# Half of an up projection rewritten as a Strassen scheme over batch pairs, its sums spread over three engines

## The chip, the cores and the metric

One core of one Trainium2 chip. Times are device microseconds of one execution. The program uses a single core, so an execution has no second core to be compared with; all runs named here agreed within 0.3% of their median unless a range is given, and the record marks all of them as fast (no run fell into a slower state that would have to be set apart). "PE" is TensorE (matmuls), "PEld" its weight loads, "DVE" VectorE, "ACT" ScalarE, "POOL" GpSimd. "L1201" in a profile line is line 1201 of the kernel's file; the lines that matter are named in words as they come.

## The reference

Eight batches of block-causal attention, and behind it a mixer with one product over tokens and one over channels:

```python
B, H, S, D = 8, 8, 576, 64                   # DM = 512, d_tok = 256, d_ch = 1536
attn = softmax(block_causal(q @ k.T / sqrt(D)))        # blocks of 64
x = (attn @ v) as (B, 576, 512)
h = relu(x.T @ w_tok1) @ w_tok2              # token mixing
u = x + h.T
h2 = relu(u @ w_ch1) @ w_ch2                 # "up" 512 -> 1536, "down" 1536 -> 512
return (u + h2).astype(float32)
```

## The kernel before

A plan in Python simulates the engines, decides once in which order every instruction is issued, and then emits them in that order; each engine runs its own queue in order. So TensorE waits wherever the next instruction of its queue isn't ready, even if a later one is. The up projection multiplies each of twelve chunks of 128 channels by the 512 columns of a batch, four matmuls of 512 columns a chunk, and one ReLU takes the result out of PSUM:

```python
sc = ring(2, [128, 2, 512], FP32, "sc", psum)   # attention's scores: two PSUM tiles of two banks
mm = ring(4, [128, 512], FP32, "mm", psum)      # everything else: four tiles of one bank
BANK = ("mm",)
def bank_of(note):
    return mm[note["slot"]]
...
def channel_up(b, uT_done, wc1_ready, prio):
    for cc in range(NDC):                        # 12 chunks
        def emit(o, cc=cc, bank=bank):
            for m in range(NDM):                 # 4 matmuls
                nc.tensor.matmul(out=bank_of(bank), lhsT=wc1_sb[:, m, channels(cc)],
                                 rhs=uT[b % 2][:, :, m, :], start=(m == 0), stop=(m == NDM - 1))
        ...
        relu(o, gT[b % 2][:, cc, :], bank_of(bank))      # ScalarE or VectorE
```

The down projection is already a seven-product (Strassen-like) scheme. Four sums of 768 bf16 columns are made on VectorE for each half batch, and seven products are folded out of PSUM one after the other:

```python
def channel_down_fast(b, g_done, wc2_ready, u_done, prio):
    for t in range(2):
        for key, dst, x, y, op in (("s1", s1, a21, a22, ADD), ("s2", s2, s1, a11, SUB),
                                   ("s4", s4, a12, s2, SUB), ("s3", a21, a11, a21, SUB)):
            nc.vector.tensor_tensor(out=dst, in0=x, in1=y, op=op)
        ...  # 7 products of 6 matmuls of 256 columns, each folded by VectorE into an fp32 tile
```

The softmax here doesn't subtract the row's maximum and nothing guards it: scores larger than these inputs give would overflow.

## Time and profile before

| | before |
|---|---|
| time, median of 3 (range) | 298.75 us (298.72 to 298.76) |
| span in the profile | 296.9 us |
| last product of attention ends | 197.9 us |
| last matmul ends | 293.5 us |
| waits of TensorE after start-up | none over 0.3 us |
| granted TensorE clock | full in all 40 slices |
| GpSimd after attention | idle |

TensorE is the bound: what it has to stream sets the end, and the other engines only have to stay out of its way. The prediction below shows the lines of the profile for that.

### The profile page before, as it was taken

The page shows a single profiled execution, that of the slowest core. Times are in us where ns is not written, and L with a number is a line of the kernel's source. Part 1 is how long each engine was busy: PE and PEld are TensorE (multiplying, and loading weights), DVE is VectorE, ACT ScalarE, POOL GpSimd, SP SyncE. Part 2 cuts the span into 40 slices and gives each one's busy share as a digit, 9 for nine tenths or more (in the row PEclk, how much of TensorE's full clock was granted, in tenths as well). Part 3 has the DMA queues.
Part 4 walks back from the last instruction along what each step waited for, and adds up shares of the span by engine and source line. Part 5 has one row for each costly group of instructions (what it writes and reads, how often), then busy time and mean ns, then how long its engine had stood idle before and what let it go on. Part 6 is the DMA issues. An engine that isn't in the chain of part 4 may idle for free.

```text
span 296.9 us, 7686 instructions
## 1 busy us (share of the span) xinstructions
PE 290.8 (98%) x3257; PEld 184.7 (62%) x3276; DVE 203.7 (69%) x509; ACT 164.4 (55%) x233; POOL 62.0 (21%) x96
## 2 busy tenths in 40 slices
PE   8999999999999999999999999999999999999995
PEld 3576456465557855546764567774586677558774
DVE  5566879899679979959988787665086085028284
ACT  5896755578767566686666664624612611670400
POOL 9776363701700070340040000000000000000000
PEclk9999999999999999999999999999999999999999
DMA  9999999992992299991239022211033043100314
GB/s 210 183 196 202 212 182 189 222 215 66 163 133 41 42 137 203 198 131 35 41 56 168 2 20 53 91 47 62 2 71 144 0 91 109 68 2 0 145 31 148
DMA packets 64387, 31.99 MB, mean 108 GB/s; under 512 B 53088, under 2 KB 55008, under 8 KB 64352
## 3 DMA queue, kind: packets, MB, share of 16 engines
q0 software_dynamic: 44320, 17.34, 49.0%
q1 hardware_dynamic: 19744, 13.57, 17.4%
q8 instruction: 25, 0.41, 0.5%
q10 hardware_dynamic: 288, 0.59, 0.5%
q14 instruction: 10, 0.08, 0.1%
HBM read 35.85 MB, written 9.44 MB: 153 GB/s over the span
## 4 chain that ended last, share of the span: by engine, by line
PE 95%; DMA 2%; DVE 1%; ACT 1%; issue 1%; ACTq 0%
PE mm L950 28%; PE mm L1049 22%; PE mm L558 10%; PE sc L511 10%; PE mm L1144 7%; PE mm L739 6%; PE mm L832 4%; PE mm L977 4%; DMA gT<-in_q_dram 2%; PE mm L863 1%; ACT e_sb L530 1%; PE mm L783 1%; PE mm L335 0%; PE mm L913 0%; DVE u_sb L847 0%
## 5 line engine op out<-in xcount | busy, mean ns | idle before, releaser
L530 ACT ACTIVATE e_sb<-sc 128x1024 bf16<-128x1024 f32 x95 | 92.6, 1028 | 30.8 <-PE sc L511 30.5
L950 PE MATMUL mm<-uT,wc_sb 128*128 128x512 bf16 x384 | 89.6, 380 | 0.0
L725 ACT ACTIVATE gT<-mm 128x512 bf16<-128x512 f32 x76 | 45.4, 597 | 64.8 <-PE mm L950 53.9
L950 PEld LDWEIGHTS <-wc_sb 128*128 128x128 bf16 x384 | 41.7, 114 | 37.1 <-issue 3.6
L425 POOL DMA_DIRECT2D v<-in_v_dram x45 | 37.1, 837 | 33.5 <-PE mm L1049 22.4
L1049 PEld LDWEIGHTS <-gT 128*128 128x128 bf16 x336 | 32.0, 98 | 6.7 <-issue 1.7
L511 PE MATMUL sc<-qT,kT 32*128 32x64 bf16 (+4 forms) x744 | 35.4, 281 | 0.4 <-DVE qT L396 0.3
L558 PEld LDWEIGHTS <-e_sb 128*128 128x128 bf16 x896 | 31.5, 97 | 6.6 <-issue 3.1
L558 PE MATMUL mm<-v,e_sb 128*128 128x65 bf16 x896 | 34.3, 193 | 0.0
L586 DVE TENSOR_TENSOR x_sb<-mm,rinv 128x320 bf16<-128x320 f32 x64 | 31.2, 491 | 2.2
L1032 DVE TENSOR_TENSOR sums<-gT 128x768 bf16<-128x768 bf16 x14 | 7.2, 555 | 36.4 <-ACT gT L725 36.4
L1071 DVE TENSOR_TENSOR o_sb<-mm,u_sb 128x256 f32<-128x256 f32 x56 | 23.1, 420 | 7.7 <-PE mm L1049 6.8
L1049 PEld LDWEIGHTS <-sums 128*128 128x128 bf16 x252 | 24.3, 98 | 5.6 <-DVE e_sb L536 0.4
L847 DVE TENSOR_TENSOR u_sb<-mm,x_sb 128x512 bf16<-128x512 f32 x28 | 17.8, 685 | 7.9 <-PE mm L832 6.6
L511 PEld LDWEIGHTS <-kT 32*128 32x128 bf16 x752 | 12.4, 93 | 17.1 <-issue 13.8
L1071 DVE TENSOR_TENSOR o_sb<-mm,o_sb 128x256 f32<-128x256 f32 x42 | 17.4, 421 | 7.5 <-PE mm L1049 7.1
L396 DVE STREAM_TRANSPOSE kT<-kraw 128x288 int32<-128x288 int32 x32 | 21.0, 705 | 1.8 <-ACT kraw L356 1.6
L1049 PE MATMUL mm<-wc_sb,gT 128*128 128x256 bf16 x168 | 22.0, 273 | 0.0
L1049 PE MATMUL mm<-wd_sb,gT 128*128 128x256 bf16 x168 | 21.9, 273 | 0.0
L1049 PE MATMUL mm<-wd_sb,sums 128*128 128x256 bf16 x168 | 21.4, 273 | 0.0
L396 DVE STREAM_TRANSPOSE qT<-qraw 128x288 int32<-128x288 int32 x32 | 21.0, 705 | 0.6 <-PE sc L511 0.3
L727 DVE TENSOR_SCALAR gT<-mm 128x512 bf16<-128x512 f32 x20 | 13.8, 688 | 7.6 <-PE mm L950 7.2
(78 smaller groups left out, 285.2 us busy)
## 6 DMA issues: line engine op xcount, KB each, us to landing
out_dram<-o_sb SPq DMA_DIRECT2D x15, 512.0 KB, 3.2
qraw<-in_q_dram POOLq DMA_DIRECT2D x15, 288.0 KB, 7.1
kraw<-in_k_dram POOLq DMA_DIRECT2D x15, 288.0 KB, 6.8
v<-in_v_dram POOLq DMA_DIRECT2D x28, 128.0 KB, 6.7
wc_sb<-in_moe_w_ch_dram POOLq DMA_DIRECT2D x8, 192.0 KB, 7.2
wc_sb<-in_moe_w_ch_dram POOLq DMA_DIRECT2D x3, 512.0 KB, 10.8
out_dram<-o_sb SPq DMA_DIRECT2D x10, 128.0 KB, 2.4
v<-in_v_dram POOLq DMA_DIRECT2D x15, 64.0 KB, 5.9
```

What stands on the lines that cost most here:

```text
L396: nc.vector.transpose(dst[:, 0:S, :] .rearrange("p s e -> p (s e)") .bitcast(I32) .rearrange("p (a k) -> p k a", k=NB)[:, k0:k1], raw2.bit ...
L425: nc.gpsimd.dma_start(out=dst, in_=src)
L511: nc.tensor.matmul(out=home(n)[:, c0 : c0 + w], lhsT=kT[i][r, j0 : j0 + 128, par], rhs=qT[i][r, i0 : i0 + w, par], start=(par == 0), stop= ...
L530: nc.scalar.activation(dst, sc[SC.index(note["pool"])][:, :, 0:n], EXP, scale=scale)
L558: nc.tensor.matmul(out=u[:, I, 0:65], lhsT=w, rhs=vt[:, J, head, 0:65], start=(J == 0), stop=(J == I),)
L586: nc.vector.tensor_tensor(out=xt[:, :, 64 * head : 64 * head + 64], in0=u[:, :, 0:64], in1=ri.to_broadcast([128, 5, 64]), op=MULT,)
L725: nc.scalar.activation(dst, src, RELU)
L739: nc.tensor.matmul(out=bank_of(bank)[:, w * n : w * n + w], lhsT=wt[:, tt : tt + 255 : 2], rhs=xt[:, c, cols], start=(c == 0), stop=(c == 4),)
L950: nc.tensor.matmul(out=bank_of(bank), lhsT=wc1_sb[:, m, channels(cc)], rhs=uT[b % 2][:, :, m, :], start=(m == 0), stop=(m == NDM - 1),)
L1049: nc.tensor.matmul(out=bank_of(bank)[:, 0:256], lhsT=x[:, kk], rhs=y[:, kk], start=first and kk == 0, stop=kk == H6 - 1, skip_group_check= ...
L1071: nc.vector.tensor_tensor(out=dst, in0=bank_of(bank)[:, 0:256], in1=other, op=ADD)
L1144: nc.tensor.matmul(out=ps, lhsT=gt[:, cc, c0 : c0 + 128], rhs=wc2_sb[:, cc, cols], start=(cc == 0 and not turned), stop=(cc == NDC - 1),)
```

## The change

Intent: take an eighth of the up projection's matmuls away for batches 4 to 7. Two batches form the two column blocks of one matrix product, and seven products of two matmuls replace eight. Four sums of weights (once) and four of the data (per pair) have to be made first, and the products have to be joined: three copies out of PSUM, three additions and some ReLUs for every group of four output chunks. The new sums lie in buffers that attention no longer needs (`raws` held the loads of q and k). To spare VectorE, GpSimd makes the weight sums, some of the down projection's sums and some residual additions; ScalarE copies for the latter. The eight PSUM banks, four of which served the scores, serve everything once the last scores are read. The diff (cuts are marked `...`):

```diff
-    qraw = ring(3, [128, NB, D], BF16, "qraw")
-    kraw = ring(3, [128, NB, D], BF16, "kraw")
+    raws = sb.tile([128, 6, NB * D], BF16, name="raws")
+    ws_sb = raws....                             # weight sums, once q and k are done with
 ...
-    BANK = ("mm",)
+    P.pool("late", [])
+    BANK = ("mm", "late")
     def bank_of(note):
-        return mm[note["slot"]]
+        n = note["slot"]
+        return mm[n] if note["pool"] == "mm" else sc[n // 2][:, n % 2]
 ...
+    def up_weight_sums(wc1_ready):
+        for dst, x, y, op in ((w[0], a21, a22, ADD), (w[1], w[0], a11, SUB),
+                              (w[2], a11, a21, SUB), (w[3], a12, w[1], SUB)):
+            def emit(o, dst=dst, x=x, y=y, op=op):
+                (nc.vector if o.engine == "DVE" else nc.gpsimd).tensor_tensor(out=dst, in0=x, in1=y, op=op)
+            prev = [P.add("POOL", 4.0, emit, deps + prev, 20.0)]                  # L1054
 ...
+    def channel_up_fast(b, uT_done, wc1_ready, prio):
+        ...                                      # 4 data sums on VectorE: L1070
+        for n in range(NDC // 2):                # 6 groups
+            # product(): 2 matmuls, L1100; keep(): copy out of PSUM, L1119; join(): L1128; clip(): ReLU in SBUF
 ...
     def channel_down_fast(...):
-                    nc.vector.tensor_tensor(out=dst, in0=x, in1=y, op=op)
+                    (nc.vector if o.engine == "DVE" else nc.gpsimd).tensor_tensor(...)    # L1201
-                    "DVE", dve_cost(768, 2), emit, ...
+                    ("DVE", "POOL") if 2 <= b < B - 1 else "DVE", ...
+                if residual and not final and FAST_UP <= b < B - 1:
+                    nc.scalar.copy(dst, bank_of(bank)[:, 0:256])                          # L1242
+                    nc.gpsimd.tensor_tensor(out=dst, in0=dst, in1=other, op=ADD)          # L1247
```

## The prediction

> **What bounds the kernel now.** I read the page first, then the chain of waits in order of time, then the waits of TensorE, then busy time by stretches, then the groups kept apart by shape.
>
> ```profile
> span 296.9 us, 7686 instructions
> PE 290.8 (98%) x3257; PEld 184.7 (62%) x3276; DVE 203.7 (69%) x509; ACT 164.4 (55%) x233; POOL 62.0 (21%) x96
> PE 95%; DMA 2%; DVE 1%; ACT 1%; issue 1%; ACTq 0%
> ```
>
> The third line is the engine summary of the chain that ended last: 95% of the span is TensorE. A busy PE alone proves little, because matmuls overlap, so I look at the spacing in the chain and at what PE waited for.
>
> ```profile
> 205.58 7.03 PE mm L950 x32
> 250.90 15.54 PE mm L950 x72
> 266.44 9.17 PE mm L1049 x84
> 286.29 7.22 PE mm L1049 x66
> PE mm L328 <- DVE wd_sb L299: 1.2, 1, 1.2
> PE sc L511 <- DVE qT L396: 0.3, 1, 0.3
> ```
>
> L950 is the up projection with 512 columns: 15.54 / 72 = 0.216 us a matmul. L1049 is the down projection, already a seven-product scheme, with 256 columns: 9.17 / 84 = 0.109 us. The last two lines are all of PE's recorded waits: 1.5 us, both at the start. So PE streams columns almost without a hole, and the time moves only if columns go away or holes appear.
>
> ```profile
> 203.00:230.00 27.00, 26.95 (x180) 17.59 (x180) 13.55 (x29) 10.53 (x18) 0.00 (x0) 1.00 0.21 59
> 230.00:260.00 30.00, 29.95 (x205) 19.81 (x204) 10.16 (x23) 12.53 (x22) 0.00 (x0) 1.00 0.25 66
> 260.00:290.00 30.00, 29.95 (x243) 22.40 (x243) 16.83 (x39) 9.18 (x16) 0.00 (x0) 1.00 0.14 45
> ```
>
> Columns: stretch, length, busy PE, PEld, DVE, ACT, POOL, granted clock, DMA share, GB/s. Attention has ended by 203 us; from there VectorE is busy 13.55 + 10.16 + 16.83 = 40.5 of 87 us (47%), ScalarE 32.2 (37%), GpSimd not at all. This is where the change puts its additions, and they have idle engines to go to.
>
> ```profile
> L725 ACT ACTIVATE gT<-mm 128x512 bf16<-128x512 f32 x76 | 45.4, 597 | 64.8 <-PE mm L950 53.9 <-DVE o_sb L1071 10.7
> L727 DVE TENSOR_SCALAR gT<-mm 128x512 bf16<-128x512 f32 x20 | 13.8, 688 | 7.6 <-PE mm L950 7.2
> L1032 DVE TENSOR_TENSOR sums<-gT,sums 128x768 bf16<-128x768 bf16 x14 | 7.4, 549 | 0.0
> L1009 DVE TENSOR_TENSOR wd_sb<-wc_sb,wd_sb 128x1536 bf16<-128x1536 bf16 x2 | 1.9, 953 | 0.0
> L1071 DVE TENSOR_TENSOR o_sb<-mm,o_sb 128x256 f32<-128x256 f32 x42 | 17.4, 421 | 7.5 <-PE mm L1049 7.1
> 200.96 2.48 DVE L847 TENSOR_TENSOR u_sb<-mm,x_sb 128x512 bf16<-128x512 f32 x4 [1.66 <-PE mm L832]
> ```
>
> These rows are the price list. The last one, from the timeline, adds one thing: four 512-column additions in a row take 2.48 us, so each costs the queue 0.62 us though one alone lasts 0.685.
>
> **What the Trainium skill says.** "TensorE: Matmul & The Clock Gate", section Back-to-back issue gap, gives N/2.4 + 2.5 ns for the warm gap: 216 ns at 512 columns. The trace agrees (215.8). "VectorE: DVE Perf Modes", section on the perf-mode tier table, caps a tensor_tensor at two elements a cycle in bf16 from SBUF and one with a PSUM operand. The trace agrees: from 768 to 1536 bf16 columns 549 becomes 953 ns (0.53 ns a column), from 256 to 512 columns out of PSUM 421 becomes 685 (1.03 ns). "GPSIMD Engine Reference", section 3.1, puts a two-input addition at about 2.6 cycles an element at 1.2 GHz; GpSimd adds nothing in this trace, so no run here shows it. "SBUF — State Buffer", section Who interferes with whom, says a VectorE instruction with two SBUF inputs and a GpSimd instruction that reads SBUF exclude each other, the later one waiting for the whole of the earlier. Nothing in this trace tests it either.
>
> **The change, part by part.**
> Removed, PE: for each of two batch pairs, two batches times 12 chunks times 4 matmuls = 96 become 6 groups of 7 products of 2 matmuls = 84. That is 2 x 12 = 24 matmuls of 512 columns less, 24 x 0.216 = **5.2 us**, all in the stage after attention, where PE is the chain. It is one eighth of half the up projection, no more: 1.7% of 298.75.
>
> Added, VectorE: per pair four sums of 1024 bf16 columns, each 0.549 + 256 x 0.00053 = 0.69 us, 5.5 us for both pairs (estimate from the two rows). Per group three joins out of PSUM, 36 in all, 36 x 0.62 = 22.3 us. Added, ScalarE or VectorE: 36 copies of a product to fp32 (0.6 us each), 12 ReLUs out of PSUM, and clips in SBUF, where the old way had 96 ReLUs. In the built order VectorE takes 10 of the 36 copies and ScalarE 26, so ScalarE stays near its old load; VectorE gains about 22.3 + 5.5 + 6.2 and a few us of clips, and loses 18 residual folds (18 x 0.41 = 7.4) and some of the down sums to ScalarE copies and GpSimd. After attention it goes from 40 to about 70 of some 85 us: over 80%.
>
> Moved: the four weight sums (1536 columns each) go to GpSimd, estimated from the skill's rate at 1536 x 2.6 / 1.2 = 3.3 us each, 13 us in a row. In the built order they follow the last transposes of raw q and k, some 36 us of PE streaming ahead of the first product that reads them. They should be hidden. The dependencies of the merged buffers are still by region: each q or k load waits for the transpose of its own slot, not for the whole merged tile.
>
> Freed: four score banks join the four general banks once the last scores are read. A group needs three banks for a chain of four products with three evictions between; 4 x 0.43 + 3 x about 0.85 = 4.3 us and a last ReLU, against 3.0 us of PE work a group. So two groups have to be in flight, six banks; with eight there is room, with four there would not be.
>
> Unchanged: the startup and attention keep their PE work, and so should the end, 3.4 us from PE's last matmul (293.5) to the end of the span, a fold and a store.
>
> Holes I expect, by walking the built order with the durations above. (a) The turn out of attention: after the last head PE has 1.7 us of products that need no sums, then token mixing of batch 7. VectorE must finish the heads (1.3 us), make the sums, two joins, a clip and a copy, and only then evicts the first token-mix banks, near 7.5 us; PE wants those banks again at 6.9. Estimate 0.8 us. (b) Inside the first pair's stage VectorE has some 25 us of work in 29, in the second pair's some 18 in 22; in-order queues at 85% will sometimes hold a bank: estimate 0.7 us. (c) The last downs: two GpSimd sums of 768 columns (768 x 2.6 / 1.2 = 1.7 us each, estimate) stand beside ten VectorE sums that PE needs in turn. If the lock is as the skill says, PE is held 0 to 2 us; I take half of it, with its slack, as 0.2 us.
>
> Sum: 298.75 - 5.2 + 0.8 + 0.7 + 0.2 = **295.2 us**.
>
> **The rivals.**
> 1. PE stays the only bound: no new holes, 298.75 - 5.2 = 293.5 us. For it: VectorE and ScalarE have idle time and a copy-join pair fits a group. Against: the load doubles on VectorE, and every group now has three PE-evict-PE turns where the old up projection had none.
> 2. VectorE becomes the bound of the two pair stages: if its additions do not overlap at 0.62 but cost 0.685, and each in-order wait on PE adds, its work in the first stage is 28 of 29 us and PE follows it. Holes of 2 to 2.5 us a stage give 298 us and the change is nearly lost.
> 3. GpSimd and VectorE exclude each other at the shared port: VectorE's sums wait behind additions of 0.8 to 1.7 us. For it: the skill. Against: most joins and folds have one PSUM operand and do not need the port. It would make 296 to 297.5 us, with the holes just ahead of L1220 in the last 50 us.
> 4. The search for an order finds another order in attention: it may win or lose a few tenths there, since PE was dense already.
>
> **Range and chances.** Under rival 1 nothing below 293.5 is to be had except from a luckier start, and 2% faster would be under 292.8; that is 0.7 us below the floor, so I give it 0.06. Slower by 2% means 304.7, eleven us of holes in a stage of 87: 0.02. Between, I put half the weight from 294 to 296, and the eight in ten from the floor, 293.4, to 297.8, which takes in rivals 2 and 3 in part.
>
> **What would show it.** Right: about 24 fewer matmuls in the up projection (168 at L1100, 192 left at L995), 0.216 us apart in their chain; the PE end moved earlier by 3 to 4 us; VectorE above 75% after attention; no PE wait on the raw weight sums; holes of under 1 us, on VectorE evictions. Wrong: PE waits of over 2 us on joins or copies (rival 2), VectorE sums at L1070 or L1201 several times longer than 0.55 to 0.69 us while GpSimd runs (rival 3), a wait for GpSimd's weight sums, or an attention stage whose end moved by more than 1 us. The prediction itself would be wrong if the span of the stage after attention shrank by over 5.5 us or by under 1.5.

## The result, and the profile after

The changed kernel is slower: **321.56 us** median of 4 runs (321.19 to 323.39; a fifth run, of 320.26, enters the ratio) against 298.74 us in the same rounds, a ratio of 1.0765 with a 95% interval of 1.0719 to 1.0811. Ratios here are the mean time of one kernel's runs over that of the other's of the same rounds, so not quite the ratio of the medians quoted. The profile below is of the slowest of these runs, 323.39 us.

The page of the changed kernel: the span, the engine summary and two rows of the 40 slices (busy tenths of TensorE, tenths of its granted clock).

```profile
span 321.2 us, 7800 instructions
PE 295.6 (92%) x3236; PEld 183.8 (57%) x3254; DVE 248.8 (77%) x547; ACT 172.7 (54%) x253; POOL 106.9 (33%) x128
PE   8999999999999999988999379998999699989695
PEclk9999999999999999999999859999999879999999
```

Fewer matmuls, yet PE's busy time went up, from 290.8 to 295.6 us, and there are holes that before did not have. The rise points at the last row: in two places the granted clock dips, so some matmuls took twice as long (those of 256 columns followed each other by 213 ns in both stretches, 109 ns outside). The clock records in the trace give the stretches: half clock from 182.5 for 10.2 us, and from 254.2 for 6.8 us. The waits of TensorE (tile, line of the waiter, engine and line waited for; us in total, times, longest):

```profile
PE mm L598 <- DVE e_sb L576: 6.6, 1, 6.6
PE mm L1220 <- DVE sums L1201: 3.8, 3, 1.4
PE sc L1220 <- DVE sums L1201: 2.0, 1, 2.0
PE sc L1100 <- ACT e_sb L396: 1.6, 5, 0.6
```

The longest is an attention product waiting 6.6 us for a memset that itself lasts 0.17 us. The timeline around it (start, length, engine, line; the bracket is idle time and its releaser) shows what the memset stood behind:

```profile
179.41 3.06 POOL L1054 TENSOR_TENSOR raws<-wc_sb 128x1536 bf16<-128x1536 bf16 x1
179.79 6.45 DVE L1201 TENSOR_TENSOR sums<-gT,sums 128x768 bf16<-128x768 bf16 x2
...
182.43 3.40 POOL L1054 TENSOR_TENSOR raws<-wc_sb,raws 128x1536 bf16<-128x1536 bf16 x1
186.32 0.17 DVE L576 MEMSET e_sb<- 64x128 uint32 x1
...
186.55 0.84 PE L598 MATMUL mm<-vals,e_sb 128*128 128x65 bf16 x12 [6.57 <-DVE e_sb L576]
```

Two VectorE sums that take 0.55 us each when alone took 3.10 and 3.43 us, one for each of the two GpSimd weight sums (3.06 and 3.40 us) beside them. VectorE's queue is in order, so the memset came after both, and TensorE after the memset. Nobody waited for the weight sums themselves: the profile lists no waiter for L1054. The windows of the stretches with the dips (busy us of PE, PEld, DVE, ACT, POOL with instruction counts, granted clock, DMA share, GB/s):

```profile
179.00:193.00 14.00, 7.43 (x105) 5.85 (x102) 11.40 (x16) 2.54 (x3) 6.83 (x3) 0.63 0.05 11
193.00:214.60 21.60, 21.49 (x296) 14.02 (x296) 13.02 (x37) 10.95 (x13) 0.00 (x0) 1.00 0.16 56
250.00:270.00 20.00, 17.01 (x133) 13.53 (x132) 13.62 (x23) 2.68 (x7) 11.43 (x12) 0.83 0.34 100
```

The sum of the loss: TensorE's last matmul ends at 317.2 us instead of 293.5, so 23.7 us later. Work saved is some 5.0 us (the built program's matmuls at their steady spacing: 274.3 us before, 269.3 after, an estimate from rows like 0.216 and 0.109 us). Holes of 0.6 us or more, counted from start to start of two matmuls beyond their steady spacing, come to 17.0 us. The half clock doubled about 6.1 us of streaming in the first stretch and 5.9 in the second, which costs half of it, 6.0 us. 17.0 + 6.0 - 5.0 leaves 5.7 us for smaller holes. The other four runs list a mean clock of 0.984 to 0.989 against 0.973 here, which is 7 to 10 us of half clock instead of 17 (an estimate from clock and span); these runs are 1.6 to 3.1 us shorter. Attention's last product ends 16.7 us later, of which 3.5 us is TensorE work that the new order places ahead of it (by the built programs, twelve matmuls of 512 columns, six of the down projection and two start-up fillers).

The chain of waits, the view that named PE for 95% of the span before, accounts for only a fifth of it here (PE 15%, DVE 4%). It was no help; the waits and the timeline were.

### The profile page after: what moved, and what is told of

It is laid out like the page before. It is cut to its first block, busy times and chain, and to the rows that moved or that the text cites. A ratio compares the mean times of both kernels' runs of the same rounds, so it can differ in the third digit from the quotient of the medians.

```text
span 321.2 us, 7800 instructions
## 1 busy us (share of the span) xinstructions
PE 295.6 (92%) x3236; PEld 183.8 (57%) x3254; DVE 248.8 (77%) x547; ACT 172.7 (54%) x253; POOL 106.9 (33%) x128
## 5 line engine op out<-in xcount | busy, mean ns | idle before, releaser
L995 PE MATMUL mm<-uT,wc_sb 128*128 128x512 bf16 x192 | 45.7, 381 | 0.2 <-ACT uT L843 0.2
L465 POOL DMA_DIRECT2D vals<-in_v_dram x45 | 37.1, 837 | 24.2 <-PE mm L1220 12.0
L436 DVE STREAM_TRANSPOSE turned<-raws 128x288 int32<-128x288 int32 x64 | 39.9, 704 | 2.9 <-ACT raws L396 1.7
L598 PEld LDWEIGHTS <-e_sb 128*128 128x128 bf16 x896 | 32.9, 99 | 13.9 <-DVE e_sb L576 7.1
L598 PE MATMUL mm<-vals,e_sb 128*128 128x65 bf16 x868 | 34.5, 196 | 6.6 <-DVE e_sb L576 6.6
L551 PE MATMUL sc<-turned 32*128 32x64 bf16 (+4 forms) x744 | 35.8, 283 | 0.3 <-DVE turned L436 0.2
L1220 PEld LDWEIGHTS <-sums 128*128 128x128 bf16 x252 | 24.8, 102 | 14.5 <-DVE sums L1201 7.1
L995 PEld LDWEIGHTS <-wc_sb 128*128 128x128 bf16 x192 | 20.5, 115 | 18.9 <-issue 2.4
L1220 PEld LDWEIGHTS <-gT 128*128 128x128 bf16 x240 | 23.5, 102 | 7.6 <-issue 3.3
L770 ACT ACTIVATE gT<-mm 128x512 bf16<-128x512 f32 x30 | 17.9, 597 | 14.2 <-PE mm L995 11.5
L1247 POOL TENSOR_TENSOR o_sb<-o_sb,u_sb 128x256 f32<-128x256 f32 x18 | 14.2, 807 | 29.5 <-ACT o_sb L1242 29.5
L1201 POOL TENSOR_TENSOR sums<-sums,gT 128x768 bf16<-128x768 bf16 x2 | 3.5, 1730 | 61.6 <-DVE sums L1201 61.6
L551 PEld LDWEIGHTS <-turned 32*128 32x128 bf16 x752 | 12.4, 93 | 16.9 <-issue 13.6
L1220 PE MATMUL mm<-wd_sb,sums 128*128 128x256 bf16 x144 | 19.3, 276 | 1.9 <-DVE sums L1201 1.4
L576 DVE MEMSET e_sb<- 64x128 uint32 (+1 forms) x72 | 10.5, 153 | 12.4 <-ACT e_sb L570 9.2
L1254 DVE TENSOR_TENSOR o_sb<-mm,o_sb 128x256 f32<-128x256 f32 x34 | 14.0, 420 | 6.0 <-PE mm L1220 5.4
```

Source lines behind the costliest of these rows:

```text
L436: nc.vector.transpose(dst[:, 0:S, :] .rearrange("p s e -> p (s e)") .bitcast(I32) .rearrange("p (a k) -> p k a", k=NB)[:, k0:k1], raw2.bit ...
L465: nc.gpsimd.dma_start(out=dst, in_=src)
L551: nc.tensor.matmul(out=home(n)[:, c0 : c0 + w], lhsT=kT[i][r, j0 : j0 + 128, par], rhs=qT[i][r, i0 : i0 + w, par], start=(par == 0), stop= ...
L598: nc.tensor.matmul(out=u[:, I, 0:65], lhsT=w, rhs=vt[:, J, head, 0:65], start=(J == 0), stop=(J == I),)
L770: nc.scalar.activation(dst, src, RELU)
L1220: nc.tensor.matmul(out=bank_of(bank)[:, 0:256], lhsT=x[:, kk], rhs=y[:, kk], start=first and kk == 0, stop=kk == H6 - 1, skip_group_check= ...
```

## The experiments

Thirteen kernels, all compared with runs of the kernel before on the same chip (298.6 to 298.74 us). Three parts of GpSimd's work can be undone without touching the order of TensorE's instructions, since the order is fixed when the plan has ended: only the engine that is called changes.

### e1, e2, e3: GpSimd's sums given back to VectorE

e1 moves the four weight sums, e2 the down sums and residual additions, e3 both.

```diff
 # e1, in up_weight_sums (L1054)        e2, in channel_down_fast (L1201, L1247)        e3: both
-    (nc.vector if o.engine == "DVE" else nc.gpsimd).tensor_tensor(out=dst, in0=x, in1=y, op=op)
+    nc.vector.tensor_tensor(out=dst, in0=x, in1=y, op=op)
```

> The changed kernel with one difference: the four weight sums of 1536 columns run on VectorE at the place in its queue that the plan had for them on GpSimd; the order on TensorE is the same to the instruction. Theory A (VectorE's two-operand sums from SBUF and GpSimd's additions exclude each other, and the hole this makes in TensorE also halves its clock): the 6.6 us hole near 180 us, the 1.5 us one before it and the first stretch of half clock (10.2 us) go away, some 11 us, against 4 x 0.95 us added to a VectorE that has room there: 309 to 312 us. Theory B (VectorE's queue is simply overfull, GpSimd is innocent): 3.8 us more on VectorE, 321 us or slower.

> The changed kernel with GpSimd's ten down sums and eighteen residual additions on VectorE at their planned places, the four weight sums still on GpSimd. Theory A (the two engines exclude each other on reads of SBUF; holes and half clock follow): the hole of over 6 us near 185 us and the 10.2 us of half clock stay, the holes at the down sums after 240 us and the second half clock go: 313 to 315 us, that is 321.6 less the 7.2 us that the same edit was worth without the weight sums (312.97 - 305.77). Theory B (VectorE overfull): slower than 321 us.

> All of GpSimd's additions (weight sums, down sums, residual additions) on VectorE at their planned places; TensorE's order unchanged. Theory A: no VectorE sum of 768 columns takes longer than 0.6 us, TensorE's waits for sums fall under 1 us, no half clock after the start: 299 to 303 us, the rest being the small holes on copies and joins. Theory B: 10 x 0.55 + 18 x 0.42 + 3.8 = 17 us more on VectorE makes it slower than 321 us.

Measured: e1 312.97 us (ratio 1.0476, 1.0458 to 1.0495), e2 312.25 us (311.11 to 313.29; 1.0453, 1.0423 to 1.0483), e3 305.77 us (1.0237, 1.0221 to 1.0252). So each part takes about 9 us away from the 321.6, and both together 15.8. The direction is Theory A's in all three; e1 and e2 lie just outside its ranges, and e3 misses 299 to 303 by 2.8 us, which stayed open until e13. The groups by shape name the mechanism. In the changed kernel:

```profile
L1201 DVE TENSOR_TENSOR sums<-gT,sums 128x768 bf16<-128x768 bf16 x8 | 13.1, 1655 | 0.0
L1054 POOL TENSOR_TENSOR raws<-wc_sb 128x1536 bf16<-128x1536 bf16 x2 | 6.5, 3250 | 10.7 <-DVE turned L436 10.7
```

and in e3:

```profile
L1201 DVE TENSOR_TENSOR sums<-gT,sums 128x768 bf16<-128x768 bf16 x10 | 5.3, 550 | 0.0
```

The same form of VectorE sum takes 1655 ns on average in the kernel with GpSimd's sums and 550 without them. These eight are the worst group: of all 46 sums at L1201 on VectorE twenty took 0.69 to 3.43 us, and each of the twenty overlapped a GpSimd addition in time (eight of them, of 1.02 us, one of the short residual additions); the other 26 took at most 0.56. VectorE doing all of them, fourteen more sums of 768 or 1536 columns and 18 more residual additions, is busy for less time (242.0 us) than VectorE helped by GpSimd (248.8 us). In e1, a weight sum on VectorE takes 0.94 us against 3.25 on GpSimd, the 6.6 us wait is down to 1.1, and the first dip of the clock is gone; the second, which stems from the down sums, remains. In e2 it is the other way round: a first dip (3.4 us) stays and the second is gone. In e3 there is no dip at all. But e3 is still 2.4% slower than before: GpSimd is not the whole story.

### e4, e5: GpSimd's work by itself, in the kernel before

The kernel before has no GpSimd sum. e4 adds 24 idle ones of 768 columns next to VectorE's down sums (the expectation says 20; it was 24), into a spare tile that nobody reads. e5 does the same with memsets of about the same length, which write but don't read (with an addition of eight columns ahead, to keep the place in the order).

```diff
 # e4                                                            # e5
+    nc.gpsimd.tensor_tensor(out=spare[768 columns],             +    nc.gpsimd.tensor_tensor(out=spare[8 columns], ...)
+                            in0=a11, in1=a12, op=ADD)           +    nc.gpsimd.memset(spare[:, 0:2032], 0.0)
```

> The kernel before, with 20 additions of 768 columns on GpSimd that nobody waits for, two at the start of each half batch of down sums (batches 2 to 6). Theory A: VectorE's down sums grow from 0.55 us to over 0.8 us on average, TensorE gets holes where it waits for them, and the time grows by 2 to 15 us though no result of GpSimd is used. Theory B: nothing waits for GpSimd, so 298.7 us as before, within 0.3 us.

> As the run with idle GpSimd additions, but each addition is one of 8 columns (for the same dependence) followed by a memset of 2032 columns, which reads nothing and should take about as long (1.7 us, estimated). If what excludes the engines is the reading of SBUF by GpSimd (theory A as the skill has it), VectorE's sums stay near 0.55 us and the time within 1 us of 298.7. If any GpSimd work in SBUF blocks VectorE's sums, it comes out like the run with additions.

Measured: e4 340.06 us (339.24 to 341.55; 1.139, 1.1354 to 1.1426), e5 299.33 us (1.0022, 1.0007 to 1.0037). Lines from the page, the waits and the groups of e4 (here L1061 are the down products, L1083 the folds, L1039 the down sums):

```profile
PEclk9999999999999999978999989998799699989979
PE mm L1061 <- DVE o_sb L1083: 21.9, 6, 5.2
L1016 POOL TENSOR_TENSOR spare<-gT 128x768 bf16<-128x768 bf16 x24 | 45.7, 1933 | 130.4 <-ACT gT L725 120.8 <-ACT e_sb L530 9.6
L1039 DVE TENSOR_TENSOR sums<-sums,gT 128x768 bf16<-128x768 bf16 x14 | 24.4, 1780 | 0.0
```

and of e5:

```profile
L1017 POOL MEMSET spare<- 128x2032 bf16 x24 | 42.9, 1788 | 0.0
L1038 DVE TENSOR_TENSOR sums<-sums,gT 128x768 bf16<-128x768 bf16 x14 | 7.2, 552 | 0.0
```

45.7 us of idle GpSimd additions cost 41 us; 42.9 us of GpSimd memsets cost 0.6. The VectorE sum of this form takes 1780 ns on average in the first and 552 in the second. These averages mix sums that had GpSimd work beside them with sums that had none, so I count the overlaps: in e5, 22 of the 56 sums overlapped a memset and none took over 0.61 us; in e4, 29 overlapped an addition, and 24 of these took 1.5 to 2.0 us. What holds VectorE is therefore what an addition does and a memset doesn't, reading SBUF; being busy and writing are not enough. (A GpSimd instruction with one input was not tried.) This and e1 to e3 establish the hold in both directions: added where it was not, and taken away where it was.

### e11: what a hole costs, by dose

The half clock was seen only beside GpSimd's sums so far. This run puts VectorE memsets that nobody waits for ahead of three mask memsets of the kernel before, no GpSimd sum anywhere.

```diff
+    doses = [(90.0, 3), (120.0, 5), (160.0, 8)]        # planned time, memsets of 2048 bf16 columns
     def mask(e, c, hs, deps, prio, urgent=0):
         def emit(o):
+            while doses and o.start > doses[0][0]:
+                for n in range(doses.pop(0)[1]):
+                    nc.vector.memset(spare, 0.0)
             nc.vector.memset(e[64:128, hs, c : c + 64], 0.0)
```

> The kernel before with three doses of idle VectorE work ahead of a mask memset of the attention, nothing reads what they write: 3 memsets of 2048 columns at about 90 us, 5 at 120 us, 8 at 160 us (from the rows of 128 and 256 words, 0.165 and 0.272 us, I estimate 0.9 us for one, so about 2.7, 4.5 and 7.3 us of delay, less what the order leaves as slack). Theory A (a hole costs more than its length once it is about 3 us long, since the clock then halves for a multiple of 3.4 us): after the first dose no granted clock below 1 and a loss of about its hole; after the third a stretch of half clock of 3.4 us or a multiple, so a loss of its hole plus 1.7 us or more; the second may fall either way. Time 298.7 + 8 to 17 us. Rival B (the half clock comes from something else in the changed kernel, as GpSimd's traffic or the mean load of TensorE): no half clock after any dose, and the time grows by the sum of the holes alone, under 12 us.

Measured: 317.88 us (316.97 to 320.08; 1.0655, 1.0619 to 1.0691). A memset took 0.912 us. The granted clock in the 40 slices, and windows around the two longer doses (columns as above):

```profile
PEclk9999999999999999899999879999999999999999
131.00:135.00 4.00, 3.16 (x59) 3.10 (x60) 3.31 (x9) 0.00 (x0) 0.53 (x1) 0.57 0.13 10
135.00:175.00 40.00, 39.65 (x472) 23.59 (x474) 32.77 (x77) 26.84 (x34) 8.41 (x10) 1.00 0.65 77
175.00:179.00 4.00, 0.52 (x3) 0.16 (x2) 3.02 (x4) 1.51 (x2) 0.00 (x0) 0.99 0.00 0
179.00:186.00 7.00, 4.15 (x26) 1.45 (x26) 5.16 (x11) 0.55 (x2) 0.00 (x0) 0.52 0.00 0
```

The first dose made two holes of 2.1 and 1.5 us with work between, and no dip. The second made a hole of 5.5 us, and half clock for 3.4 us; the third one of 6.5 us, and half clock for 6.8 us, of which about 3.9 fell on streaming. So holes bring the half clock with no GpSimd sum anywhere. The holes sum to 15.6 us; the half clock adds (2.8 + 3.9) / 2 = 3.4; together 19.0, and TensorE's last matmul is 18.3 us later. The median is 2.2 us over the expected range; the rival, no half clock and under 12 us, is out.

How long the dip lasts is not fixed by the hole: the same hole of 6.6 us was followed by 10.2 us in the profiled run of the changed kernel and 6.8 in e12 below, and the clocks listed for the other runs of the changed kernel differ too. In all these runs the stretches before the last matmul were 3.4, 6.8 or 10.2 us.

### e6: what the joins cost

e6 is e3 without the copies, joins and clips of the new scheme: a ScalarE ReLU stands in for each join. Its output is wrong, which doesn't matter for the time.

```diff
-    cast(o, dst, bank_of(bank))                                                     # keep
+    pass
-    nc.vector.tensor_tensor(out=dst, in0=bank_of(bank), in1=src, op=ADD)            # join
+    nc.scalar.activation(dst, bank_of(bank), RELU)
-    ... tensor_scalar_max / RELU in SBUF                                            # clip
+    pass
```

> Wrong result on purpose. The run with all additions on VectorE, less the bookkeeping of the up scheme: the copies of products to fp32 and the clips are left out, each join becomes a plain ReLU out of PSUM on ScalarE; TensorE's order is the same. It prices the joins, copies and clips. Rival 2 (joins and copies hold banks): the 6 us of small holes in the two pair stages shrink to under 2, giving 299 to 301 us against 305.8. If the holes came from the order of the products itself, it stays at 305 us.

Measured: 301.26 us (1.0087, 1.007 to 1.0104). Of e3's 7 us, 4.5 hang on the joins, copies and clips, nearly what rival 2 asked for (299 to 301). That didn't say whether by their length or by something that they wait on, and the rest stayed open.

### e7, e8: the same change, planned without GpSimd

e3's order had been planned for a GpSimd that helps. e7 tells the plan that all sums are VectorE's; e8 does so with one batch pair only (6 and 7).

```diff
 # e7
-            prev = [P.add("POOL", 4.0, emit, deps + prev, 20.0)]
+            prev = [P.add("DVE", dve_cost(1536, 2), emit, deps + prev, 20.0)]
-                    ("DVE", "POOL") if 2 <= b < B - 1 else "DVE",
+                    "DVE",
-                if residual and not final and FAST_UP <= b < B - 1:
+                if False:                       # no ScalarE copy and GpSimd addition
 # e8: e7, and
-    FAST_UP = 4
+    FAST_UP = 6
```

> The seven-product up projection for batches 4 to 7 as in the change, but the plan is told that every sum is VectorE's: weight sums, down sums and residual folds; GpSimd only issues DMAs, and the search places them. Theory A: with no exclusion the order behaves as planned, no half clock, holes of 1 to 3 us in all: 295 to 298 us, a little faster than before. Theory B (VectorE overfull with 36 joins): holes of over 5 us, slower than 300 us.

> As the replanned run, with the up scheme for batches 6 and 7 alone (12 matmuls of 512 columns fewer, 2.6 us). Theory A: half the saving with half the joins: 296 to 297.5 us, between the kernel before and the replanned two pairs. Theory B: it beats the two-pair version because VectorE has half the extra load.

Measured: e7 301.28 us (1.0084, 1.0069 to 1.0099), e8 301.28 us (1.0087, 1.0072 to 1.0102). Better than e3, and still no gain, for one pair as for two. Theory A is missed by over 3 us in both. For e7 both figures of Theory B came: slower than 300 us, and 6.9 us lost by TensorE after attention (99.3 us for 92.4 us of work at steady spacing). Whether its cause holds, a VectorE with too much to do, e9 decides. The waits of TensorE in e7 after 190 us:

```profile
PE sc L1220 <- DVE o_sb L1254: 1.2, 3, 0.9
PE sc L1100 <- DVE vals L1128: 1.0, 1, 1.0
PE sc L1100 <- DVE o_sb L1254: 0.5, 1, 0.5
PE sc L1100 <- DVE gT L1128: 0.4, 1, 0.4
PE sc L1100 <- DVE e_sb L398: 0.4, 1, 0.4
PE mm L1100 <- ACT gmT L770: 0.3, 1, 0.3
```

All but the last are on `sc`, and so is one more of 0.2 us that is left out, though the products use the four `mm` banks as much. The built program says why. I followed each wait of a product to the instruction that releases it, and told the two banks of an `sc` tile apart by their offset:

```
PE#6026  L1100 writes sc1 bank 1   waits for  DVE#587  L1128 (a join)   which reads sc1 bank 0
PE#6066  L1100 writes sc0 bank 0   waits for  DVE#599  L398  (a copy)   which reads sc0 bank 1
PE#6330  L1220 writes sc0 bank 1   waits for  DVE#636  L1254 (a fold)   which reads sc0 bank 0
PE#6466  L1220 writes sc1 bank 1   waits for  DVE#658  L1254 (a fold)   which reads sc1 bank 0
```

The plan treats the four banks as independent. The dependency tracking of the framework treats each two-bank tile as one. In the kernel before it made no difference, as one activation reads both banks of a score tile and nothing else uses them.

### e9, e10: a tile for each bank

When attention has read its last scores, the two-bank tile is given back and two tiles of one bank take its bytes. Nothing else changes; the order of all instructions is the one of e7 (e8).

```diff
-    sc = ring(2, [128, 2, 512], FP32, "sc", psum)
+    sc_pools = [tc.alloc_tile_pool(name=f"sc{f}", bufs=1, space=PSUM, side=side) for f, side in ...]
+    sc = [sc_pools[f].tile([128, 2, 512], FP32, name=f"sc{f}") for f in range(2)]
+    late = [None, None]
     def bank_of(note):
-        return mm[n] if note["pool"] == "mm" else sc[n // 2][:, n % 2]
+        if note["pool"] == "mm":
+            return mm[n]
+        f = n // 2
+        if late[f] is None:
+            sc_pools[f].release()
+            sc_pools[f] = tc.alloc_tile_pool(name=f"late{f}", bufs=1, space=PSUM, side=..., reuse_waits="tile")
+            late[f] = [sc_pools[f].tile([128, 512], FP32, name=f"late{2 * f + i}") for i in range(2)]
+        return late[f][n % 2]
```

> Same order of every instruction as e7 (planner told that GpSimd takes no sums, two batch pairs), but when the attention is done with one of the two PSUM tiles of two banks for its scores, that tile is given back and two tiles of one bank take its bytes, so that a product into one bank no longer waits for VectorE's reader of its neighbour. In e7 the built program holds such waits (a product into bank 1 of a tile waiting for the join that reads bank 0), and nearly all of its waits of TensorE after 212 us are on those two tiles. Theory A (the coupled banks are what e7 lost to its plan): the waits on these banks fall from about 5 us to under 2, time 295 to 298, that is 0.985 to 0.998 of before, below before for the first time. Rival B (the sums themselves lag: VectorE's queue of joins is behind anyway, and the neighbour's reader only happened to be the last named): the same waits move to the bank's own reader, time 300 to 302.

> e8 (one batch pair, 6 and 7, in the Strassen form; the others as before) with the same change of banks as e9. It saves half of the 24 matmuls, some 2.6 us of TensorE. Theory A: 296 to 298.5, a little over e9 as less is saved. Rival B: as e8, 301. If e9 falls and this one does not, the loss of e8 is in its tail (the mixed rows' stores come last), which the banks do not touch.

Measured, both correct: **e9 295.38 us** (295.23 to 296.22; ratio 0.9897, 0.9882 to 0.9911), e10 297.59 us (0.9964, 0.995 to 0.9977). Both are faster than the kernel before, e9 by 1.0% and e10 by 0.4%, with intervals clear of 1. The span of e9, its waits of TensorE after 190 us (all that are listed), and its first window after attention:

```profile
span 293.5 us, 7741 instructions
PE mm L1112 <- ACT gmT L782: 0.3, 1, 0.3
PE mm L1339 <- issue: 0.2, 1, 0.2
196.00:230.00 34.00, 33.80 (x213) 18.95 (x214) 32.09 (x62) 16.92 (x27) 0.00 (x0) 1.00 0.21 45
```

The waits on those banks went from the 3.5 us listed for e7 to nothing, and the time fell by 5.9 us; the other 2.4 us are in gaps that this view doesn't list. That settles it between the theories: had VectorE's queue been late by itself, the products would have waited for their own bank's reader. VectorE is indeed 94% busy in that window (32.09 of 34 us), and TensorE still streams for 33.80.

### e12, e13: the four corners, in the changed kernel's own order

e12 is the changed kernel with the banks apart, e13 is e3 with the banks apart (edits as above).

> The changed kernel with one edit: the scores' PSUM tiles of two banks are given back after attention and tiles of one bank take their bytes (as e9); GpSimd keeps all its sums, TensorE's order is the changed kernel's own. If the two causes add up (GpSimd's holds, coupled banks): about 316 to 319, that is 3 to 5 us under the changed kernel. If the coupling is hidden under GpSimd's holds, or the holds' half clock swallows it: 320 to 322. If the banks were the main cause after all: under 312.

> e3 (all of GpSimd's sums on VectorE, TensorE's order as in the changed kernel) with the banks apart. If the coupled banks are what e3 still lost after attention: 299.5 to 302.5 (e3 305.8; of its 7 us, 3.5 are TensorE work that this order places before the last attention product and VectorE's ready work there, which the banks do not touch). If VectorE's queue itself is the limit in this order, as GpSimd's sums were planned away from it: 304 to 306.

Measured: e12 315.7 us (315.19 to 316.06; 1.0564, 1.0548 to 1.058), e13 298.95 us (298.42 to 299.09; 1.0003, 0.999 to 1.0015).

| same TensorE order, median us | banks as one tile of two | a tile for each bank |
|---|---|---|
| GpSimd makes sums | 321.56 (the changed kernel) | 315.70 (e12) |
| VectorE makes all sums | 305.77 (e3) | 298.95 (e13) |

GpSimd costs 15.8 or 16.8 us, the coupled banks 5.9 or 6.8: they add up, within 1 us. e12's expectation had a little less for the banks (3 to 5 us), e13's was 299.5 to 302.5; both lost slightly more to the banks than I had thought. The waits of e12 keep the mark of GpSimd:

```profile
PE mm L610 <- DVE e_sb L588: 6.6, 1, 6.6
PE mm L1232 <- DVE sums L1213: 3.8, 3, 1.4
```

e13's order was planned for a helping GpSimd; planning anew for VectorE alone (e9) takes off another 3.6 us. In e13 attention's last product ends at 203.9 us, in e9 at 196.0; the placed work differs by 5.7 us in the same direction, so about 2.2 of these 8 us are waits that e9 doesn't have there.

## Why the prediction was wrong, point by point

- **TensorE's saving, 5.2 us: right.** The built program has 168 matmuls at L1100 and 192 at L995, as the prediction said, 24 fewer than the 384 before (and two more of start-up filler), some 5.0 us at steady spacing. e9 and e10 turn a part of it into time: two pairs 3.2 us, one pair 1.0. On the price of a matmul: the section of the Trainium skill that the prediction cites ("TensorE: Matmul & The Clock Gate", Back-to-back issue gap) gives its formula for an isolated matmul, and about 131 ns for one of 512 columns in a stream. Here the stream itself took 215.8 ns a matmul, and the measurement decides.
- **The step that failed: "They should be hidden."** I had asked when the weight sums' results were needed, found 36 us of slack, and priced them at nothing. The results were indeed early: nobody waited for them. But the weight sums, 3.3 us each on GpSimd by my estimate (measured 3.06 to 3.45), held the VectorE sums beside them, the last two for their whole length; behind these sums in VectorE's queue stood a mask memset, and TensorE waited for the memset: 6.6 us in one piece, in attention, where I had looked for nothing. Moving these four instructions alone to VectorE brings 8.6 us (e1).
- **Rival 3 was the right mechanism with the wrong size and place.** I gave the exclusion 296 to 297.5 us and put its holes "just ahead of L1220 in the last 50 us", with "additions of 0.8 to 1.7 us"; hole (c) of my sum, 0.2 us for two GpSimd sums of 768 columns, is its term. Taking all of GpSimd's sums away brings 15.8 us (e3). I left the longest GpSimd instructions out of the rival, and counted only those VectorE instructions that exclude directly; a fold out of PSUM keeps its own length beside GpSimd (420 ns in e4 as before), but stands in the same queue.
- **What no term of the sum had: the half clock.** Holes were priced at their length. Of 23.7 us of delay in the profiled run about 6 come from streaming at half clock after holes. e11 shows that holes do it without GpSimd's sums.
- **"With eight there is room": wrong as built.** I checked the merged SBUF tiles for false waits, not the PSUM tiles. Four of the eight banks were tied in two pairs, at a cost of 5.9 us (after against e12) to 6.8 us (e3 against e13).
- **Rival 2 (VectorE's load): no.** I estimated 70 of 85 us after attention. In e9, which gives VectorE the sums of GpSimd too, it is 84.6 of 93 us, and what TensorE loses there is 0.8 us (93.2 us from attention's last product to the last matmul, 92.4 of work at steady spacing). In-order queues at 91% did hold, once nothing else held them.
- **Hole (a), 0.8 us at the turn out of attention: the right size by luck.** There is a wait of 0.6 us (a hole of 0.75) at 222.7 us, of a token-mixing product for VectorE's eviction, as I had it. But the built program has that product write bank 0 of an `sc` tile and wait for the reader of bank 1, and with the banks apart (e12, and e13 against e3) the hole is gone. It was the coupled banks, not VectorE's work at the turn.
- **The falsifiers.** I had written that VectorE sums several times longer than 0.55 us, or an attention stage whose end moved by over 1 us, would tell against me. Both came (two sums of 3.1 and 3.4 us and nine of 1.2 to 2.2; 16.7 us).

The way from the changed kernel to e9 is 26.2 us, nearly the prediction's error of 26.4: 15.8 for GpSimd's sums (e3), 6.8 for the coupled banks (e13), 3.6 for an order planned without GpSimd (e9). That e9's 295.38 is so near the 295.2 of the prediction is in part luck: in e9 GpSimd makes no sums at all, and the 1.7 us of holes in the prediction's sum are not e9's (0.8 us after attention). The kernel that was built is not that version, and what was to be known beforehand I had not followed up in two places: which of VectorE's sums stand beside GpSimd's longest instructions, and whose readers a product into a bank waits for.

## What to carry to other kernels

A helper engine's instruction is not hidden because its result is early: ask which queue it stops while it runs, and what stands in that queue behind. Give independent uses independent tiles, also in PSUM, and read the built program's waits for neighbours that wait for each other. And price a hole of several microseconds in front of TensorE above its length, as streaming at half clock follows.

## What the Trainium skill lacked or had wrong

- "SBUF — State Buffer", section Who interferes with whom, says that a VectorE instruction with two SBUF inputs contends with a GpSimd instruction that reads SBUF and not with one that only writes. The runs agree: 24 additions on GpSimd cost 41 us (e4), 24 memsets of the same length 0.6 us (e5). What it lacks is the price: the held VectorE instruction stops its in-order queue, so TensorE waited 6.6 us for a memset of 0.17 us that GpSimd's additions do not lengthen (in the changed kernel three such memsets ran beside them, in 0.165 us each).
- "GPSIMD Engine Reference", section 3.1: about 2.6 cycles an element agreed (1536 columns 3.06 to 3.45 us, 768 columns 1.6 to 2.0 us). Its comparison with VectorE is for fp32, 1.96 times slower; for the bf16 sums here it lacks the larger factor, about 3.5 (VectorE made the same 1536 columns in 0.94 us in e1). Nor does it say that giving VectorE all of these sums can lower VectorE's own busy time, here from 248.8 to 242.0 us (e3).
- "TensorE: Matmul & The Clock Gate", the summary's row on avoiding throughput drops, asks for no idle gap of over about 3 us, and Part 1 gives a free-running window of 3413 ns. The stretches of 3.4, 6.8 and 10.2 us agree with the window. But two gaps of 1.2 and 2.2 us, 2.8 us apart from end to end, were enough (half clock for 6.8 us in the changed kernel, 3.4 in e1 and in e12), while gaps of 2.1 and 1.5 us, 4.0 us apart, were not (e11): a single gap of that length is not needed. (The page's section "A second HAM failure mode: psum-queue depth-cycling" does say that frequent short idles bring the half clock, without saying how long or how close.)
- "PSUM — Partial Sum Buffer", section PSUM bank collisions raise a hardware error, has the rule to guard PSUM by bank and quadrant, or more simply by bank. Nothing there says that a tile of two banks may be guarded as one; here that cost 5.9 to 6.8 us.
